# Handing the first DFT stage to the second by one-partition SBUF-to-SBUF DMAs instead of through DRAM

## The chip, the cores and the metric

The kernel runs on one core of one Trainium2 chip. The metric is the device time of one execution in microseconds (us). The median of three timed executions before the change is 1575.53 us (1574.32 to 1576.95). A difference below about 0.2% (3 us) can't be told from no change.

## The reference

Two blocks follow each other: a filter along the sequence, done in the frequency domain, and a gated feed-forward network.

```python
# x: (8, 3136, 256); filt_r, filt_i: (1569, 256)
X = np.fft.rfft(x, axis=1)
y = np.fft.irfft(X * (filt_r + 1j * filt_i)[None], n=3136, axis=1)
# w_in: (256, 1024), conv_w: (3, 1024), w_out: (1024, 256)
h = np.maximum(y @ w_in, 0)
conv_out = sum(conv_w[k] * hp[:, k:k + 3136] for k in range(3))   # hp: h with a zero row at both ends
out = (h * sigmoid(conv_out)) @ w_out
```

## The kernel before, in words

**The transform.** 3136 = 112 x 28, so the transform of a batch is made of matmuls with DFT tables. A *step* works on 2 of the 28 columns; 14 steps (`NP`) make a batch and 112 steps the eight batches. In one step there are:

- `first(b, p)`: loads rows of `x` (tile `x`, 112 x 512 floats, 224 KB), multiplies by `s1_sb` (two matmuls, L321), and `store("sa", ...)` copies the result from PSUM with ScalarE to the tile `sa` (L309) and sends it by a DMA on ScalarE's queue (L315) to the DRAM tensor `a_dram[b]`. A partition of `sa` holds one of 4 row kinds r and one of 28 groups g; the free axis has the 2 columns of the step.
- `second(b, p)`: needs, on the partitions, all 28 columns n and the 4 kinds r, and on the free axis the groups g. So `load("a", b, p)` reads `a_dram[b]` back in another order (on SyncE's queue, SP; L304), 2 groups a step. That is a turn of the data: each step of `second` needs something of every step of `first` of its batch. `second` multiplies by `s2_sb` (L328; in the last step of a batch L331) into PSUM `pp`.
- `filt(b, p)`: VectorE multiplies by the filter (L340 to L342), GpSimd adds (L344) into `z`.
- `third(b, p)`: multiplies `z` by `i1_sb` (L351); `store("sb", ...)` copies with ScalarE and sends it to `b_dram`.

`last_load`, `last_stage` and `last_out` bring `b_dram` back (tile `br`), make the last matmul (L216) and split the result in two parts, `y`, for the network. For batch 0 this happens at the end of this forward loop, for the others inside the network.

**The order.** One loop over `i` writes the instructions of PE, ACT, DVE and POOL in the order in which they run. In iteration `i` stand `first` of step `i - 1`, `second` of step `i - SKEW - 1`, `filt` of step `i - SKEW - 2` and `third` of step `i - SKEW - 4`, with `SKEW = NP + 4` = 18: the second stage runs 18 steps behind the first. DMAs on SP follow the order of the source as their waits allow. In the same loop, `x` is loaded 7 steps ahead, the tables and the filter are loaded in the first 26 iterations, and `convert_weights` turns the 64-bit weights into 32-bit pairs, a few instructions per iteration, in 8 chunks of 512 words from each weight tensor.

**DMA completions.** All DMAs of SP and ACT share eight completion semaphores, given out in turn (`DMAHW0` to `DMAHW7` in the rows below). A DMA that takes a semaphore waits until the DMA that had it before, eight places back in the order of both queues together, has landed.

**The network.** After the loop come the 28 chunks of the network (`inner`, `relu`, `conv`, `gate`, `split_g`, `project`), which fill the larger part of the span. The change doesn't touch them.

Of the kernel before, what the change touches and what calls it, by code (L numbers as in the profile page):

```python
# [9 lines left out]
F32 = mybir.dt.float32  # L10
F32R = mybir.dt.float32r
I32 = mybir.dt.int32
U32 = mybir.dt.uint32
AF = mybir.ActivationFunctionType
# [4 lines left out]
N2 = 28  # L19
G = 28  # L20
D = 256
# [17 lines left out]
def _dft_tables():  # L39
# [7 lines left out]
    n1, n2, c, a = np.arange(N1), np.arange(N2), np.arange(N2), np.arange(N1)  # L47
    s1 = np.zeros((N1, N2, 112))
    m2 = np.zeros((112, N1))
    i1 = np.zeros((2, 2, 28, G, N2, 4))  # L50
    for g in range(G):
        for s in range(2):
            if g == G - 1 and s == 1:
# [6 lines left out]
                for j in range(14):  # L60
                    if j:
                        w = np.conj(_w(j * c, N2))
                        i1[0, s, j, g, :, 2] = 2 * w.real
                        i1[1, s, j, g, :, 2] = -2 * w.imag
                    w = np.conj(_w((56 + 112 * j) * c, S))
# [4 lines left out]
            w = _w(k1 * (28 * n1[:, None] + n2[None, :]), S)  # L70
            s1[:, :, 2 * s * 28 + g] = w.real
            s1[:, :, (2 * s + 1) * 28 + g] = w.imag
            w = np.conj(_w(k1 * a, N1))
            m2[2 * s * 28 + g] = 2 * w.real / S
            m2[(2 * s + 1) * 28 + g] = -2 * w.imag / S
            for j in range(28):
                k2, sg = (j, 1) if j < 14 else (41 - j, -1)
                w = np.conj(_w((k1 + 112 * k2) * c, S))
# [5 lines left out]
    def s2(special):  # L84
        m = np.zeros((112, 2, 2, 28))
        for s in range(2):
            for j in range(28):
                if special and s == 1:
                    if j == 0:
                        m[n2 * 4 + 2, 0, s, 0] = 1.0  # L90
                        m[n2 * 4 + 2, 1, s, 0] = (-1.0) ** n2
                    else:
                        w = _w(n2 * j, N2) if j < 14 else _w(n2 * (56 + 112 * (j - 14)), S)
                        r = 2 if j < 14 else 3
                        m[n2 * 4 + r, 0, s, j] = w.real
                        m[n2 * 4 + r, 1, s, j] = w.imag
                    continue
                k2, sg = (j, 1) if j < 14 else (41 - j, -1)
                w = _w(n2 * k2, N2)
                m[n2 * 4 + 2 * s, 0, s, j] = w.real  # L100
                m[n2 * 4 + 2 * s + 1, 0, s, j] = -w.imag
                m[n2 * 4 + 2 * s, 1, s, j] = sg * w.imag
                m[n2 * 4 + 2 * s + 1, 1, s, j] = sg * w.real
        re, im, gap = m[:, 0].reshape(112, 56), m[:, 1].reshape(112, 56), np.zeros((112, 8))
        return np.concatenate([re, gap, im, -im, gap, re], 1)

    i1 = i1.reshape(2, 56, G, 112)
    i1 = np.concatenate([i1[0], np.zeros((8, G, 112)), i1[1]])
# [16 lines left out]
def tile_fft_filter_gated_ffn(  # L125
# [16 lines left out]
    nc = tc.nc  # L142
    B = x.shape[0]
# [35 lines left out]
        nc.tensor.matmul(ps, lhsT=wl, rhs=rh, start=False, stop=stop, **kw)  # L179

    dram = ctx.enter_context(tc.tile_pool(name="dram", bufs=1, space=bass.MemoryType.DRAM))
    a_dram = [dram.tile([N2, 112, D], F32, name=f"a_dram{b}") for b in range(B)]
    b_dram = [dram.tile([N2, 112, D], F32, name=f"b_dram{b}") for b in range(B)]

    wc = ctx.enter_context(tc.tile_pool(name="wc", bufs=1))
# [4 lines left out]
    wi = [wc.tile([128, KT, FF], F32R, name=f"wi{h}") for h in range(2)]  # L190
    wo = [wc.tile([128, NF, D], F32R, name=f"wo{h}") for h in range(2)]
# [33 lines left out]
    forward_pools = ExitStack()  # L225
    xp = forward_pools.enter_context(tc.tile_pool(name="xp", bufs=2, side="right"))
    s1_sb = xp.tile([112, N2, 112], F32, name="s1_sb", bufs=1)
    with (
        tc.tile_pool(name="fc", bufs=1) as fc,
        tc.tile_pool(name="fp", bufs=2) as fp,  # L230
# [3 lines left out]
        s2_sb = fc.tile([112, 120], F32, name="s2_sb")  # L234
        s2s_sb = fc.tile([112, 120], F32, name="s2s_sb")
# [5 lines left out]
        t1_sb = fc.tile([120, G, D], F32, name="t1_sb")  # L241
        t2_sb = fc.tile([120, G, D], F32, name="t2_sb")

        rows = {}

        def load_filter(c):
# [11 lines left out]
        raws = {}  # L258

        def load_weights(k):  # L260
            raws[k] = raw = cv.tile([128, 2, 512], I32, name="raw")
            for part, src in enumerate((w_in, w_out)):
                nc.sync.dma_start(out=raw[:, part], in_=src[:, 512 * k:512 * k + 512])

        def convert_conv():
            n = 3 * NF
            raw = cv.tile([128, 2, 512], I32, name="raw")
            nc.sync.dma_start(out=raw[:, 0, 0:2 * n], in_=conv_w)
            yield
            em = cv.tile([128, 2, 512], I32, name="em", bufs=1)  # L270
            yield from to_f32(cw.rearrange("p k f -> p (k f)"), raw[:, 0, 0:2 * n], em[:, 0, 0:n], em[:, 1, 0:n])

        def convert_weights():

            for k in range(8):
                raw = raws.pop(k)
                em = cv.tile([128, 2, 512], I32, name="em", bufs=1)
                ws = cv.tile([128, 2, 256], F32, name="ws")
                yield from to_f32(ws.rearrange("p t n -> p (t n)"), raw.rearrange("p t n -> p (t n)"), em[:, 0], em[:, 1])
                yield  # L280
                parts = [[t.rearrange("p a b -> p (a b)")[:, 256 * k:256 * k + 256] for t in w] for w in (wi, wo)]
                for part, (wh, wl) in enumerate(parts):
                    hi_act(wh, ws[:, part])
                yield
                for part, (wh, wl) in enumerate(parts):
                    lo_pool(wl, ws[:, part], wh)
                    yield
                if k < 6:
                    load_weights(k + 2)

        NP = 14
        parts = {}
        psums = {}

        def pool(kind):
            return xp if kind in ("x", "sa") else fp

        def load(kind, b, p):
            r = pool(kind).tile([112, 2, D], F32, name=kind, bufs=8 if kind == "x" else 5)
            if kind == "x":  # L300
                v = x[b].rearrange("(p n) d -> p n d", n=N2)
            else:
                v = a_dram[b].rearrange("n (r g) d -> (n r) g d", g=G)
            nc.sync.dma_start(out=r, in_=v[:, 2 * p:2 * p + 2])  # L304
            rows[kind, b, p] = r

        def store(kind, b, p, ps):
            st = pool(kind).tile([112, 2, D], F32, name=kind, bufs=4)
            nc.scalar.activation(st, ps, AF.Copy)  # L309
            sl = slice(2 * p, 2 * p + 2)  # L310
            if kind == "sa":
                v = a_dram[b][sl].rearrange("n p d -> p n d")
            else:
                v = b_dram[b].rearrange("n (r g) d -> (n r) g d", g=G)[:, sl]
            nc.scalar.dma_start(out=v, in_=st)  # L315

        def first(b, p):
            r = rows.pop(("x", b, p))
# [3 lines left out]
            return ps  # L322

        def second(b, p):
            r = rows.pop(("a", b, p))
            pp = fps.tile([120, 2, D], F32, name="pp", bufs=3)
            if p < NP - 1:
                nc.tensor.matmul(pp, lhsT=s2_sb, rhs=r, start=True, stop=True)  # L328
            else:
                for j, m in ((0, s2_sb), (1, s2s_sb)):  # L330
                    nc.tensor.matmul(pp[:, j], lhsT=m, rhs=r[:, j], start=True, stop=True)  # L331
            psums[b, p] = pp
# [21 lines left out]
        def at(i):  # L354
            return divmod(i, NP) if 0 <= i < NP * B else None

        SKEW = NP + 4
        nc.sync.dma_start(out=s1_sb[:, 0:4], in_=s1[:, 0:4])
        load("x", 0, 0)
        load("x", 0, 1)  # L360
        for c in range(1, 4):
            nc.sync.dma_start(out=s1_sb[:, 4 * c:4 * c + 4], in_=s1[:, 4 * c:4 * c + 4])
            load("x", 0, 2 * c)
            load("x", 0, 2 * c + 1)
        csteps, wsteps = convert_conv(), convert_weights()
        done = NP * B + 6
        NI = max(NP * B + SKEW + 5, done + N2 // 2 + 3)
        with tc.manual_schedule(engines=COMPUTE):
            for i in range(NI):
                f, m = i, i - SKEW  # L370
                if i == done:
                    forward_pools.close()
                    yps.append(ctx.enter_context(tc.tile_pool(name="y_even", bufs=1, side="right", reuse_waits="tile")))
                    lp = ctx.enter_context(tc.tile_pool(name="lp", bufs=2, side="right", reuse_waits="tile"))
                if 1 <= i < 4:
                    nc.sync.dma_start(out=s1_sb[:, 4 * i + 12:4 * i + 16], in_=s1[:, 4 * i + 12:4 * i + 16])
                if (bp := at(f + 7)) and i:
                    load("x", *bp)
                if bp := at(m + 3):
                    load("a", *bp)  # L380
                if i == 6:
                    nc.sync.dma_start(out=s2_sb, in_=s2[:, 0:120])
                    nc.sync.dma_start(out=s2s_sb, in_=s2s[:, 0:120])
                    nc.sync.dma_start(out=m2_sb, in_=m2)
                if 12 <= i < 26 and i % 2 == 0:
                    sl = slice((i - 12) // 2 * 4, (i - 12) // 2 * 4 + 4)
# [4 lines left out]
                pt = third(*bp) if (bp := at(m - 4)) else None  # L391
                pf = first(*bp) if (bp := at(f - 1)) else None
                if bp := at(m - 1):
                    second(*bp)
                if pt is not None:
                    store("sb", *at(m - 4), pt)
                if pf is not None:
                    store("sa", *at(f - 1), pf)
                if 3 <= i < 16:
                    next(csteps, None)  # L400
                if i == 16:
                    load_weights(0)
                    load_weights(1)
                if i >= 22 and i % 9 != 8:
                    next(wsteps, None)
                if 16 <= i < 30 and i % 2 == 0:
                    copy_filter(i // 2 - 8)
                c = 2 * (i - done)
# [113 lines left out]
                evacuate(*a)  # L522


PLAG = 6
AVOID = (3, 4, 5, 6, 7)
COMPUTE = {mybir.EngineType.PE, mybir.EngineType.Activation, mybir.EngineType.DVE, mybir.EngineType.Pool}
# [38 lines left out]
```

## Time and profile before

| What | Value |
|---|---|
| timed executions | 1574.32, 1575.53, 1576.95 us |
| span of the profiled execution | 1573.9 us (1.6 us below the median of the timed ones) |
| PE busy | 1510.8 us (96%) |
| DVE, ACT, POOL busy | 1280.7, 1192.6, 698.0 us |
| mean granted clock of TensorE | 0.984 |
| HBM read, written | 88.03 MB, 77.07 MB |
| `a_dram<-sa`, `a<-a_dram` | 112 DMAs each, 224 KB each |

The profile shows one execution. Its span runs from the first to the last instruction; what lies around it in a timed execution is the difference to the time. An engine's busy time is no bound by itself: the forward stage (to about 385 us) and the network (from there) have different limits and are read apart. For a DMA, "issue" is the time that the issuing queue (SPq, ACTq) spends on the instruction, and "landing" the time from the issue's start to the completion.

### The profile page before, as it was taken

Reading aid. Unit: us, or ns where it says so; the run is one execution under the profiler, and the core shown is the slowest. Engines: PE = TensorE matmul, PEld = TensorE weight load, DVE = VectorE, ACT = ScalarE, POOL = GpSimd, SP = SyncE. Lnnn points to the kernel's source line nnn. Section 1 sums busy time; section 2 is a strip of 40 time slices with the busy share of each in tenths; the row PEclk is TensorE's granted clock in tenths of the full one; section 3 lists DMA queues with packets and bytes.
Section 4 is the critical chain, followed back from the end, with each engine's and each line's share of the span. In section 5 each row is a group of like instructions: output and inputs, shape, how many; then the busy total and the mean of one; then the engine's idle time right before and its main releaser. Section 6 shows DMA issues by size and latency. Waiting matters only on the chain.

```text
span 1573.9 us, 26330 instructions
## 1 busy us (share of the span) xinstructions
PE 1510.8 (96%) x9424; PEld 1351.0 (86%) x9424; DVE 1280.7 (81%) x1965; ACT 1192.6 (76%) x2162; POOL 698.0 (44%) x624
## 2 busy tenths in 40 slices
PE   5699999998999999999999999999999999999998
PEld 4366666656999999999999999999999999999998
DVE  0487878897888888888888888888888888888887
ACT  3444444445988888888888888888888888888887
POOL 0255555562444444444444444444444444444444
PEclk8699999999999999999999999999999999999999
DMA  9999999984111011111111111111111111100001
GB/s 292 298 345 349 341 309 338 340 251 142 30 48 48 30 48 48 48 48 48 40 33 36 47 48 49 46 48 47 36 42 48 48 37 41 48 24 25 24 24 48
DMA packets 128278, 166.83 MB, mean 106 GB/s; under 512 B 10682, under 2 KB 87571, under 8 KB 128147
## 3 DMA queue, kind: packets, MB, share of 16 engines
q1 hardware_dynamic: 86931, 113.74, 23.1%
q10 hardware_dynamic: 41216, 51.39, 9.9%
q8 instruction: 75, 1.23, 0.3%
q14 instruction: 56, 0.46, 0.1%
HBM read 88.03 MB, written 77.07 MB: 105 GB/s over the span
## 4 chain that ended last, share of the span: by engine, by line
PE 83%; DMA 9%; DVE 4%; ACT 2%; issue 1%; ACTq 0%; POOL 0%; SPq 0%; DVEq 0%; POOLq 0%
PE ps_h L178 12%; PE ps_h L179 12%; PE ps_h L177 11%; PE po L473 11%; PE po L475 11%; PE po L474 11%; PE ps_h L216 5%; PE ps L321 4%; DMA x<-in_x 3%; PE ps L351 3%; PE pp L328 3%; DMA a<-a_dram 2%; DMA a_dram<-sa 2%; DVE y L149 1%; DVE v L341 1%
## 5 line engine op out<-in xcount | busy, mean ns | idle before, releaser
L152 POOL TENSOR_TENSOR g<-t,g 128x448 fp32r<-128x448 f32 x448 | 517.6, 1156 | 667.6 <-ACT g L146 265.8
L473 PE MATMUL po<-wo,g 128*128 128x256 f32 x1568 | 441.5, 282 | 0.0
L475 PE MATMUL po<-wo,g 128*128 128x256 f32 x1568 | 433.8, 277 | 0.0
L474 PE MATMUL po<-wo,g 128*128 128x256 f32 x1568 | 433.4, 276 | 0.0
L447 DVE SCALAR_TENSOR_TENSOR t<-ps_h,cw,t 128x448 f32<-128x448 f32 x448 | 305.5, 682 | 83.9 <-ACT t L442 73.3
L178 PE MATMUL ps_h<-y,wi 128*128 128x450 f32 x896 | 330.8, 369 | 4.2 <-DVE y L149 4.2
L177 PE MATMUL ps_h<-y,wi 128*128 128x450 f32 x896 | 329.2, 367 | 3.4 <-ACT y L146 2.1
L179 PE MATMUL ps_h<-y,wi 128*128 128x450 f32 x896 | 329.2, 367 | 0.0
L448 DVE SCALAR_TENSOR_TENSOR t<-ps_h,cw,t 128x448 f32<-128x448 f32 x448 | 306.4, 684 | 16.0
L442 ACT ACTIVATE t<-ps_h,cw 128x448 f32<-128x448 f32 x448 | 285.2, 637 | 42.1 <-ACT ps_h L440 0.7
L473 PEld LDWEIGHTS po<-wo,g 128*128 128x128 f32 x1568 | 294.7, 188 | 7.0
L474 PEld LDWEIGHTS po<-wo,g 128*128 128x128 f32 x1568 | 294.3, 188 | 5.7
L475 PEld LDWEIGHTS po<-wo,g 128*128 128x128 f32 x1568 | 294.4, 188 | 0.0
L440 ACT ACTIVATE ps_h<-ps_h 128x450 f32<-128x450 f32 x448 | 251.6, 562 | 32.5 <-PE ps_h L179 27.7
L453 DVE TENSOR_TENSOR t<-ps_h,t 128x448 f32<-128x448 f32 x448 | 275.1, 614 | 0.1
L452 ACT ACTIVATE t<-t 128x448 f32<-128x448 f32 x448 | 255.1, 569 | 12.2 <-DVE t L448 11.0
L146 ACT ACTIVATE g<-t 128x448 fp32r<-128x448 f32 x448 | 254.4, 568 | 0.2 <-DVE t L453 0.2
L344 POOL TENSOR_TENSOR z<-u,v 120x512 f32<-120x512 f32 x112 | 157.2, 1404 | 169.5 <-DVE v L342 144.8
L177 PEld LDWEIGHTS ps_h<-y,wi 128*128 128x128 f32 x896 | 170.4, 190 | 12.0 <-ACT y L146 3.3
L179 PEld LDWEIGHTS ps_h<-y,wi 128*128 128x128 f32 x896 | 168.6, 188 | 13.9
L178 PEld LDWEIGHTS ps_h<-y,wi 128*128 128x128 f32 x896 | 168.6, 188 | 13.5 <-DVE y L149 6.6
L149 DVE TENSOR_TENSOR y<-ps_h,y 128x448 fp32r<-128x448 f32 x98 | 103.1, 1052 | 76.7 <-ACT y L146 76.7
(51 smaller groups left out, 1447.5 us busy)
## 6 DMA issues: line engine op xcount, KB each, us to landing
x<-in_x SPq DMA_DIRECT2D x112, 224.0 KB, 4.6
a_dram<-sa ACTq DMA_DIRECT2D x112, 224.0 KB, 4.5
a<-a_dram SPq DMA_DIRECT2D x112, 224.0 KB, 4.7
b_dram<-sb ACTq DMA_DIRECT2D x112, 224.0 KB, 4.1
br<-b_dram SPq DMA_DIRECT2D x112, 224.0 KB, 2.6
out<-ot SPq DMA_DIRECT2D x27, 896.0 KB, 4.1
raw<-in_w_in SPq DMA_DIRECT2D x8, 256.0 KB, 4.6
raw<-in_w_out SPq DMA_DIRECT2D x8, 256.0 KB, 5.3
```

Of the source, the lines that this page charges most:

```text
L152: nc.gpsimd.tensor_tensor(out=dst, in0=src, in1=hi.bitcast(F32), op=ALU.subtract)
L177: nc.tensor.matmul(ps, lhsT=wh, rhs=rh, start=start, stop=False, **kw)
L178: nc.tensor.matmul(ps, lhsT=wh, rhs=rl, start=False, stop=False, **kw)
L179: nc.tensor.matmul(ps, lhsT=wl, rhs=rh, start=False, stop=stop, **kw)
L442: nc.scalar.activation(t, h[:, 1:SUB + 1], AF.Copy, scale=cw[:, 1, f:f + 1])
L447: nc.vector.scalar_tensor_tensor(out=t, in0=h[:, 0:SUB], scalar=cw[:, 0, f:f + 1], in1=t, op0=ALU.mult, op1=ALU.add)
L448: nc.vector.scalar_tensor_tensor(out=t, in0=h[:, 2:SUB + 2], scalar=cw[:, 2, f:f + 1], in1=t, op0=ALU.mult, op1=ALU.add)
L452: nc.scalar.activation(t, t, AF.Sigmoid)
L453: nc.vector.tensor_mul(t, h[:, 1:SUB + 1], t)
L473: nc.tensor.matmul(o, lhsT=gh[:, sl], rhs=wo[0][:, f], start=first, stop=False, skip_group_check=True)
L474: nc.tensor.matmul(o, lhsT=gh[:, sl], rhs=wo[1][:, f], start=False, stop=False, skip_group_check=True)
L475: nc.tensor.matmul(o, lhsT=gl[:, sl], rhs=wo[0][:, f], start=False, stop=last, skip_group_check=True)
```

## The change

The DRAM tensors `a_dram` go. Two SBUF tiles, `a_even` and `a_odd` (112 x 28 x 256 floats each), hold a whole batch in the order that `second` needs, and `second` reads its two groups right out of them. `load("a", ...)` goes. After `first` has been copied to `sa`, the new `turn` issues eight DMAs for the step, one for each pair of column j and kind r: each takes 28 partitions of `sa`, 1 KB from each, and writes the 28 KB into one partition of the batch tile. Six of the eight go out on SP and two on ACT (`BY_SP = 6`). The row that a DMA writes is `14 * (2 * r + j) + p`, so the eight rows of a step are 14 partitions apart; the rows of the table `s2` are put in the same order. `SKEW` becomes `NP + 2`. To make room in SBUF, `x` has 7 buffers instead of 8 and is loaded 5 steps ahead, and the weights are converted in 16 chunks of half the size, two pieces an iteration.

```diff
-        return np.concatenate([re, gap, im, -im, gap, re], 1)
+        rows = np.array([14 * (2 * r + n % 2) + n // 2 for n in range(28) for r in range(4)])
+        out = np.zeros((112, 120))
+        out[rows] = np.concatenate([re, gap, im], 1)
+        return out
...
-    a_dram = [dram.tile([N2, 112, D], F32, name=f"a_dram{b}") for b in range(B)]
...
+    a_sb = [xp.tile([112, G, D], F32, name="a_even", bufs=1)]
...
+        a_sb.append(fc.tile([112, G, D], F32, name="a_odd"))
...
-            raws[k] = raw = cv.tile([128, 2, 512], I32, name="raw")
+            raws[k] = raw = cv.tile([128, 2, 256], I32, name="raw")
...
-            for k in range(8):
+            for k in range(16):
...
+        def store_a(b, p, ps):
+            st = xp.tile([112, 2, D], F32, name="sa", bufs=4)
             nc.scalar.activation(st, ps, AF.Copy)
-            sl = slice(2 * p, 2 * p + 2)
-            if kind == "sa":
-                v = a_dram[b][sl].rearrange("n p d -> p n d")
...
-            nc.scalar.dma_start(out=v, in_=st)
+            rows["sa", b, p] = st
+
+        def turn(engine, b, p, which):
+            for q in which:
+                j, r = divmod(q, 4)
+                row = 14 * (2 * r + j) + p
+                engine.dma_start(out=a_sb[b % 2][row:row + 1], in_=rows["sa", b, p][28 * r:28 * r + 28, j])
...
         def second(b, p):
-            r = rows.pop(("a", b, p))
+            r = a_sb[b % 2][:, 2 * p:2 * p + 2]
...
-        SKEW = NP + 4
+        SKEW = NP + 2
...
-        done = NP * B + 6
+        done = NP * B + 4
...
-                if (bp := at(f + 7)) and i:
-                    load("x", *bp)
-                if bp := at(m + 3):
-                    load("a", *bp)
+                if (bp := at(f + 5)) and i:
+                    load(*bp)
...
+                if bp := at(f - 2):
+                    turn(nc.sync, *bp, range(BY_SP))
+                    turn(nc.scalar, *bp, range(BY_SP, 8))
+                    del rows["sa", bp[0], bp[1]]
...
-                if i >= 22 and i % 9 != 8:
+                if i >= 22:
+                    next(wsteps, None)
                     next(wsteps, None)
...
+BY_SP = 6
...
-    nc = bacc.Bacc("TRN2", target_bir_lowering=False, num_devices=1)
+    nc = bacc.Bacc("TRN2", target_bir_lowering=False, num_devices=1, dynamic_dma_scratch_size=1024)
```

SP's queue in the middle of the forward stage, before: each step has one load of `x` and one of `a`. The names in brackets are what a row waits for: a completion semaphore, or an engine.

```order
L304 DMA x<-in_x 112x512 [waits DMAHW7_49,PE_49]
L304 DMA a<-a_dram_61 112x512 [waits DMAHW0_49,PE_49]
L304 DMA x<-in_x 112x512 [waits DMAHW2_49,PE_49]
L304 DMA a<-a_dram_61 112x512 [waits DMAHW4_49,PE_49]
L304 DMA x<-in_x 112x512 [waits DMAHW6_49,PE_49]
```

The same queue after (two steps):

```order
L301 DMA x<-in_x 112x512 [waits DMAHW5_49,PE_49]
L313 DMA a_odd<-sa 1x28x256 [waits DMAHW6_49,Activation_49]
L313 DMA a_odd<-sa 1x28x256 [waits DMAHW0_49]
L313 DMA a_odd<-sa 1x28x256 [waits DMAHW2_49]
L313 DMA a_odd<-sa 1x28x256 [waits DMAHW4_49]
L313 DMA a_odd<-sa 1x28x256 [waits DMAHW5_49]
L313 DMA a_odd<-sa 1x28x256 [waits DMAHW6_49]
L301 DMA x<-in_x 112x512 [waits DMAHW7_49,PE_49]
L313 DMA a_odd<-sa 1x28x256 [waits DMAHW0_49,Activation_49]
```

One load of `a` has gone out of each step and six small DMAs have come in, each of which waits for a completion semaphore; `x` now stands behind them.

ACT in the same place, before:

```order
L309 ACTIVATE sb<-ps 112x512 [waits PE_49]
L315 DMA b_dram_69<-sb 112x512 [waits DMAHW4_49,Activation_49]
L309 ACTIVATE sa<-ps 112x512 [waits PE_49]
L315 DMA a_dram_62<-sa 112x2x256 [waits DMAHW6_49,Activation_49]
```

ACT after:

```order
L313 DMA a_odd<-sa 1x28x256 [waits DMAHW5_49,Activation_49]
L313 DMA a_odd<-sa 1x28x256 [waits DMAHW7_49]
L317 ACTIVATE sb<-ps 112x512 [waits PE_49]
L318 DMA b_dram_61<-sb 112x512 [waits Activation_49]
L306 ACTIVATE sa<-ps 112x512 [waits DMAHW3_49,DMAHW4_49,DMAHW2_49,DMAHW6_49,DMAHW0_49,PE_49]
```

Two small DMAs with a wait each now stand ahead of the copy of `sb` in a step, and the copy of `sa` waits for the DMAs that read the same buffer four steps before.

More of the change, by code (lines that the diff above doesn't have):

```diff
@@ L260, in load_weights @@
         def load_weights(k):
-            raws[k] = raw = cv.tile([128, 2, 512], I32, name="raw")
+            raws[k] = raw = cv.tile([128, 2, 256], I32, name="raw")
             for part, src in enumerate((w_in, w_out)):
-                nc.sync.dma_start(out=raw[:, part], in_=src[:, 512 * k:512 * k + 512])
+                nc.sync.dma_start(out=raw[:, part], in_=src[:, 256 * k:256 * k + 256])
         def convert_conv():
             n = 3 * NF
-            raw = cv.tile([128, 2, 512], I32, name="raw")
+            raw = cv.tile([128, 2, 256], I32, name="raw")
             nc.sync.dma_start(out=raw[:, 0, 0:2 * n], in_=conv_w)
             yield
-            em = cv.tile([128, 2, 512], I32, name="em", bufs=1)
+            em = cv.tile([128, 2, 256], I32, name="em", bufs=1)
             yield from to_f32(cw.rearrange("p k f -> p (k f)"), raw[:, 0, 0:2 * n], em[:, 0, 0:n], em[:, 1, 0:n])
         def convert_weights():
-            for k in range(8):
+            for k in range(16):
                 raw = raws.pop(k)
-                em = cv.tile([128, 2, 512], I32, name="em", bufs=1)
-                ws = cv.tile([128, 2, 256], F32, name="ws")
+                em = cv.tile([128, 2, 256], I32, name="em", bufs=1)
+                ws = cv.tile([128, 2, 128], F32, name="ws")
                 yield from to_f32(ws.rearrange("p t n -> p (t n)"), raw.rearrange("p t n -> p (t n)"), em[:, 0], em[:, 1])
                 yield
-                parts = [[t.rearrange("p a b -> p (a b)")[:, 256 * k:256 * k + 256] for t in w] for w in (wi, wo)]
+                parts = [[t.rearrange("p a b -> p (a b)")[:, 128 * k:128 * k + 128] for t in w] for w in (wi, wo)]
                 for part, (wh, wl) in enumerate(parts):
@@ L287, in convert_weights @@
                     yield
-                if k < 6:
+                if k < 14:
                     load_weights(k + 2)
@@ L293, in tile_fft_filter_gated_ffn, with load, store_b @@
         psums = {}
[L295 to L308, printed above, removed]
-            nc.scalar.activation(st, ps, AF.Copy)
-            sl = slice(2 * p, 2 * p + 2)
-            if kind == "sa":
-                v = a_dram[b][sl].rearrange("n p d -> p n d")
-            else:
-                v = b_dram[b].rearrange("n (r g) d -> (n r) g d", g=G)[:, sl]
-            nc.scalar.dma_start(out=v, in_=st)
+        def load(b, p):
+            r = xp.tile([112, 2, D], F32, name="x", bufs=7)
+            nc.sync.dma_start(out=r, in_=x[b].rearrange("(p n) d -> p n d", n=N2)[:, 2 * p:2 * p + 2])
+            rows["x", b, p] = r
+        def store_a(b, p, ps):
+            st = xp.tile([112, 2, D], F32, name="sa", bufs=4)
+            nc.scalar.activation(st, ps, AF.Copy)
+            rows["sa", b, p] = st
[4 more added lines that the diff above has]
+                engine.dma_start(out=a_sb[b % 2][row:row + 1], in_=rows["sa", b, p][28 * r:28 * r + 28, j])
+        def store_b(b, p, ps):
+            st = fp.tile([112, 2, D], F32, name="sb", bufs=4)
+            nc.scalar.activation(st, ps, AF.Copy)
+            nc.scalar.dma_start(out=b_dram[b].rearrange("n (r g) d -> (n r) g d", g=G)[:, 2 * p:2 * p + 2], in_=st)
         def first(b, p):
@@ L355, in at @@
             return divmod(i, NP) if 0 <= i < NP * B else None
-        SKEW = NP + 4
+        SKEW = NP + 2
         nc.sync.dma_start(out=s1_sb[:, 0:4], in_=s1[:, 0:4])
-        load("x", 0, 0)
-        load("x", 0, 1)
-        for c in range(1, 4):
+        load(0, 0)
+        load(0, 1)
+        for c in range(1, 3):
             nc.sync.dma_start(out=s1_sb[:, 4 * c:4 * c + 4], in_=s1[:, 4 * c:4 * c + 4])
-            load("x", 0, 2 * c)
-            load("x", 0, 2 * c + 1)
+            load(0, 2 * c)
+            load(0, 2 * c + 1)
         csteps, wsteps = convert_conv(), convert_weights()
-        done = NP * B + 6
+        done = NP * B + 4
         NI = max(NP * B + SKEW + 5, done + N2 // 2 + 3)
@@ L374, in tile_fft_filter_gated_ffn @@
                     lp = ctx.enter_context(tc.tile_pool(name="lp", bufs=2, side="right", reuse_waits="tile"))
-                if 1 <= i < 4:
-                    nc.sync.dma_start(out=s1_sb[:, 4 * i + 12:4 * i + 16], in_=s1[:, 4 * i + 12:4 * i + 16])
-                if (bp := at(f + 7)) and i:
-                    load("x", *bp)
-                if bp := at(m + 3):
-                    load("a", *bp)
+                if 1 <= i < 5:
+                    nc.sync.dma_start(out=s1_sb[:, 4 * i + 8:4 * i + 12], in_=s1[:, 4 * i + 8:4 * i + 12])
+                if (bp := at(f + 5)) and i:
+                    load(*bp)
                 if i == 6:
-                    nc.sync.dma_start(out=s2_sb, in_=s2[:, 0:120])
-                    nc.sync.dma_start(out=s2s_sb, in_=s2s[:, 0:120])
+                    nc.sync.dma_start(out=s2_sb, in_=s2)
+                    nc.sync.dma_start(out=s2s_sb, in_=s2s)
                     nc.sync.dma_start(out=m2_sb, in_=m2)
@@ L394, in tile_fft_filter_gated_ffn @@
                     second(*bp)
+                if bp := at(f - 2):
+                    turn(nc.sync, *bp, range(BY_SP))
+                    turn(nc.scalar, *bp, range(BY_SP, 8))
+                    del rows["sa", bp[0], bp[1]]
                 if pt is not None:
-                    store("sb", *at(m - 4), pt)
+                    store_b(*at(m - 4), pt)
                 if pf is not None:
-                    store("sa", *at(f - 1), pf)
+                    store_a(*at(f - 1), pf)
                 if 3 <= i < 16:
```

## The prediction, made before the changed kernel was run

> **What bounds the kernel now.** I read the page's slices first, since the change touches one stage only.
>
> ```profile
> span 1573.9 us, 26330 instructions
> ...
> PE   5699999998999999999999999999999999999998
> ...
> PEclk8699999999999999999999999999999999999999
> DMA  9999999984111011111111111111111111100001
> GB/s 292 298 345 349 341 309 338 340 251 142 30 48 48 30 48 48 48 48 48 40 33 36 47 48 49 46 48 47 36 42 48 48 37 41 48 24 25 24 24 48
> ```
>
> A slice is 39 us. The DMA digits stand at 8 or 9 for nine slices, to about 350 us, and fall to 1 when the network starts. PE stands at 9 from the third slice on. So whatever this change does, it does in the first quarter of the span; the network (about 1185 us) stays as it is. The middle of the forward stage in the view by windows, and after it in the view by tile the DMAs' issue times (ns, least/median/most) and the start of the first and last one:
>
> ```profile
> core 0: us, PE busy (x) PEld busy (x) DVE busy (x) ACT busy (x) POOL busy (x), PEclk, DMA share, GB/s
> 80.00:320.00 240.00, 224.72 (x845) 148.45 (x844) 196.69 (x296) 106.04 (x183) 135.56 (x104) 0.99 1.01 336
> ```
>
> ```profile
> L315 ACTq DMA_DIRECT2D a_dram<-sa x112: 311/312/1102, 7.1 to 327.6; - x112
> L304 SPq DMA_DIRECT2D a<-a_dram x112: 303/311/1352, 38.3 to 359.5; - x112
> L315 ACTq DMA_DIRECT2D b_dram<-sb x112: 310/321/386, 60.4 to 383.7; - x112
> ```
>
> The 112 stores of `sa` run from 7.1 to 327.6 us: 320.5 / 111 = 2.89 us a step. The window therefore holds 240 / 2.89 = 83 steps, and a step takes PE 224.72 / 83 = 2.71 us, DVE 2.37, ACT 1.28, POOL 1.63. The DMA engines are at a share of 1.01 with 336 GB/s: four transfers of 224 KB a step (0.917 MB / 2.89 us = 317 GB/s, and the rest weights and filters). So two things are at their limit together, the DMA engines and, 0.18 us below, PE. What the step waits for is shown by the waits of SP's own queue between 80 and 340 us (total, times, longest):
>
> ```profile
> SPq L304 <- PE ps L321: 55.6, 46, 2.2
> SPq L304 <- PE pp L328: 29.0, 30, 2.5
> SPq L304 <- DMA x<-in_x: 25.5, 31, 2.4
> SPq L304 <- DMA a<-a_dram: 22.9, 29, 3.6
> SPq L304 <- DMA a_dram<-sa: 20.0, 16, 3.4
> ```
>
> SP waits some 85 us for PE to free a buffer and some 68 us for DMAs (the first two rows, the last three). Both sorts are there: when DMAs are late PE stands, and the other way round. The stage would gain at most what lies between 2.89 and 2.71 us a step if all DMA trouble went.
>
> **What goes.** Two 224 KB transfers a step, 51.4 MB in all, and SP's one issue of `a` (0.31 us). On the DMA engines three transfers of 224 KB stay a step instead of four, one of them now from SBUF to SBUF. If bytes were all that counts, a step would need 3 x 0.229 MB / 336 GB/s = 2.05 us of them, which is under PE's 2.71.
>
> **What comes: issue time.** A step issues 7 DMAs on SP (`x`, six of `turn`) and 3 on ACT (`sb`, two of `turn`). Rows for one issue:
>
> ```profile
> L256 SPq DMA_DIRECT2D t_sb<-in_nyq x1: 229/229/229, 89.2 to 89.2; - x1
> ```
>
> ```profile
> 15.01 0.31 SPq L304 DMA_DIRECT2D x<-in_x  x1
> 15.37 0.43 SPq L376 DMA_DIRECT2D s_sb<-in_s  x1
> ```
>
> The only one-partition DMA (1 KB) took 0.23 us to issue, a large one 0.31, and the next one began 0.36 us after the one before. I take 0.36: SP needs 7 x 0.36 = 2.5 us a step, ACT 1.28 + 3 x 0.36 - these issues don't count as busy - = 2.4 us. Both stay under PE's 2.71, but SP goes from a queue with much spare time to one with 0.2 us of it. At 0.23 an issue SP would need 2.0 us. No cost on the path by itself.
>
> **What comes: the wait for a completion.** All DMAs share eight completion semaphores in turn, so at most eight are in flight. Before, a step had 4 DMAs, so a DMA had two steps (5.8 us) to land. Now a step has 10 and a DMA has 0.8 of a step. The step can't be shorter than the sum of the ten times to landing divided by 8. What a DMA takes to land, when the queues are full and when they are less so (medians of the DMA view: the page, then the windows 360 to 380 us at 172 GB/s, and 320 to 345 us at 234 GB/s):
>
> ```profile
> x<-in_x SPq DMA_DIRECT2D x112, 224.0 KB, 4.6
> ...
> out<-ot SPq DMA_DIRECT2D x1, 128.0 KB, 2.2
> ```
>
> ```profile
> br<-b_dram SPq DMA_DIRECT2D x7, 224.0 KB, 2.7
> b_dram<-sb ACTq DMA_DIRECT2D x6, 224.0 KB, 2.2
> ```
>
> ```profile
> b_dram<-sb ACTq DMA_DIRECT2D x10, 224.0 KB, 2.9
> a<-a_dram SPq DMA_DIRECT2D x10, 224.0 KB, 3.5
> ```
>
> After the change some 0.69 MB move in a step of about 3.3 us, 208 GB/s, between the two windows: I take 2.5 us for `sb` and 3.1 for `x`, 5.6 together. For one of the eight small ones no row exists, so from both sides. Low: the store of 224 KB in the quiet window lands in 2.2 us, of which 0.229 MB / 336 GB/s = 0.7 is transfer; 1.5 is left, and 28 KB at full rate add 0.1: 1.6 us. With the half of the 0.7 us that lie between the two windows for load, 1.95. High: all 28 KB go into one partition. If a partition takes them no faster than one DMA engine moves data (336 / 16 = 21 GB/s), that is 1.37 us instead of 0.1; on the 128 KB row's base (2.2 - 0.4 = 1.8) it makes 3.2, and with load 3.55. I take 2.5: the rows nearest to it in path and size of a packet give 1.95, and some of the one-partition cost must be paid, though eight DMAs go to eight partitions and can overlap.
>
> [...]
>
> **The sum.** (5.6 + 8 x 2.5) / 8 = 3.2 us, and 0.05 us between a landing and the next issue (the gap between the two issues above), ten times a step over eight, makes 3.26; I say 3.3. That is 0.41 us more than 2.89, times 112 steps: +46 us. `SKEW` falls by 2, so the tail after the last `first` has two iterations less. That tail ran from 327.6 to some 386 us, 23 iterations of 2.5 us: -5 us. Start-up: before, 18 iterations passed before `second` began, now 16, but SP has 16 x 2.5 = 40 us of issues in them plus some 30 loads of tables and filters at about 0.4 us, 52 us; 18 x 2.89 = 52. Nothing gained there. Forecast +41 us on the span of 1573.9 us, which lies 1.6 us below the median; on the median, 1616.5 us.
>
> **Edits at nothing.** The weights in 16 chunks: DVE's seven pieces and POOL's and ACT's few come twice as often at half the size.
>
> ```profile
> L168 DVE SCALAR_TENSOR_TENSOR ws<-em 128x512 f32<-128x512 int32 x7 | 4.8, 693 | 0.2
> L170 DVE TENSOR_SCALAR em<-ws 128x512 int32<-128x512 int32 x7 | 3.0, 428 | 0.2
> ```
>
> Seven such pieces a chunk are 7 x 0.43 to 7 x 0.69, about 4 us, and 8 chunks 32 us. If a half took as long as a whole (the worst), 32 us more over some 95 iterations: DVE at 2.37 + 0.34 = 2.71 us a step, still under 3.3. That cover is gone if the step falls to 2.7: then DVE is level with PE. `x` 5 steps ahead instead of 7 is 16 us ahead, against 3 us to land. The row order of `s2` changes no instruction. `turn` of a batch's first step waits for `second` of the last step two batches before, behind which `x` is queued; PE is ahead of SP when SP sets the pace, so I give it nothing. In the other case it costs a fraction of a step, eight times. Who waits when a small DMA is late: on ACT the copies of `sb` and `sa` behind it, for these PE, which has five PSUM buffers to run ahead.
>
> **Rivals.**
> - *The hand-over is fast (faster).* If a small DMA lands in 1.95 us, the sum gives (5.6 + 15.6) / 8 + 0.06 = 2.7 us, and PE with 2.71 sets the step. 96 steps past start-up x 0.18 = 17 us, and the tail's 5: -22, so about 1555 us. For it: the DMA engines' need falls from a share of 1.0 to 2.05 / 2.71 = 0.76, so landings shorten for all, and the wait for `a_dram` goes. Against it: 10 landings a step on 8 semaphores leave 2.1 us each, and no row is lower than 2.2. It decides below a landing of about 2.2 us, where the step is 2.94 and the loss is just the tail's 5 us.
> - *No change.* Landings of 2.1 to 2.2 us, or a step held at 2.9 by SP's issues with its waits: within 3 us of 1575.5.
> - *The small DMAs go one after the other (much slower).* If a small DMA is spread over many engines which all write the same partition, and the next one comes behind it on the same engines, none may overlap; then a step takes 8 x 1.37 = 11 us, and the kernel (11 - 2.89) x 112 = 910 us more. Against it: eight different partitions, and SP issues them 0.36 us apart, so engines that are done can go on. [...]
>
> **How the numbers follow.** Slower by a step of 3.0 to 4.3 us: 0.52, with the likeliest at 1616 us and a range of its own of 1585 to 1728. One after the other: 0.05. Fast hand-over: 0.37. No change: 0.06. So faster 0.37, same 0.06, slower 0.57. The range from 1553 (PE's floor) to 1720 us (a landing of 3.5) leaves out the case of one after the other, the top of the slow case and a gain beyond the floor.
>
> **What would show it.** [...] I am wrong if the small DMAs land in under 2.2 us, or if the start-up, which I hold at 52 us, gets much shorter because the stores to DRAM no longer compete with the loads there.

## The result, and the profile after

The changed kernel takes 1986.3 us (median of four, 1981.9 to 1988.9) against 1576.2 us: 1.260 times as long, interval 1.258 to 1.262. The forecast was 1616 us, with a range to 1720. The sign was right, the size was not: +410 us instead of +41. The page of the profile after, its span and slices (50 us each):

```profile
span 1983.9 us, 27237 instructions
...
PE   4165647475645538999999999999999999999999
...
PEclk6576778676877769999999999999999999999999
DMA  4455444344444435011111111111111111110101
```

The forward stage now fills 16 slices, 800 us. PE mostly stands at 4 to 7 there, and the DMA engines at 4 instead of 9: neither is at a limit. The granted clock of PE is lower there too (0.75 between 150 and 700 us), but PE is busy for 311 of these 550 us, and SP's own waits for PE add up to 3.5 us in them, so a slow PE isn't what SP waits for. The view by tile shows the issues of the small DMAs on SP and the copies of `sa`:

```profile
L313 SPq DMA_DIRECT2D a_even<-sa x336: 741/756/1534, 9.0 to 657.9; - x168
L306 ACT ACTIVATE sa<-ps x112: 597/597/598, 6.2 to 725.0; 112x512 f32<-112x512 f32 x112
...
L301 SPq DMA_DIRECT2D x<-in_x x112: 312/369/638, 1.2 to 700.0; - x112
```

The copies start 718.8 / 111 = 6.48 us apart (before: 2.89). One small DMA takes 0.756 us to issue, where a large one before took 0.31. SP's timeline in the middle of the stage (start, length):

```profile
409.63 0.37 SPq L301 DMA_DIRECT2D x<-in_x  x1
410.10 4.79 SPq L313 DMA_DIRECT2D a_even<-sa  x6
415.46 0.34 SPq L301 DMA_DIRECT2D x<-in_x  x1
415.90 4.74 SPq L313 DMA_DIRECT2D a_even<-sa  x6
```

Six issues fill 4.8 us, 0.80 us each with the gap, and the step is 5.8 us long although SP hardly waits in it. What it waits for between 150 and 700 us (84 steps):

```profile
SPq L301 <- DMA a_odd<-sa: 22.9, 25, 2.0
SPq L313 <- DMA b_dram<-sb: 20.9, 6, 4.4
SPq L301 <- DMA a_even<-sa: 17.1, 19, 1.9
```

All rows of this view make 92 us, 1.1 us a step. So of a step of 6.5 us in that window about 4.5 are issues of small DMAs, 0.5 the issues of `x` and of the weights, 0.4 gaps, and 1.1 waits. The whole +410 us is 3.59 us a step times 111 = 398, and 12 us in the tail: from the last `sa` to the last `sb` 68 us now (725.0 to 793.1), 56 before. The page holds no time to landing for the small DMAs of this kernel, so whether they land in under 2.2 us, where the prediction calls itself wrong, can't be read from it.

Some of the waits stand at one place: `second` of a batch's first step needs the last small DMA of the batch, and SP is behind. PE stood from 368.1 to 388.5 us ahead of that `second` (L331), and the matmuls of L354 and L324 that follow it in the program ran only after it, from 390.3. VectorE's timeline at such a place (the bracket is the idle time before):

```profile
362.85 0.69 DVE L345 TENSOR_TENSOR v<-pp,t_sb 56x512 f32<-56x512 f32 x1
390.63 0.69 DVE L343 TENSOR_TENSOR u<-pp,t_sb 120x512 f32<-120x512 f32 x1 [27.09 <-PE pp L331]
```

For 27 us the second stage stands; `sa` stands there for one step of 11 to 12 us in each batch.

### The profile page after: what moved, and what is told of

Read it like the earlier page. It is cut to its first block, busy times and chain, and to the rows that moved or that the text cites. A ratio compares the mean times of both kernels' runs of the same rounds, so it can differ in the third digit from the quotient of the medians.

```text
span 1983.9 us, 27237 instructions
## 1 busy us (share of the span) xinstructions
PE 1611.3 (81%) x9424; PEld 1382.6 (70%) x9424; DVE 1322.9 (67%) x2021; ACT 1193.2 (60%) x2178; POOL 689.5 (35%) x648
## 4 chain that ended last, share of the span: by engine, by line
PE 59%; DVE 2%; SPq 1%; DMA 1%; ACT 1%; issue 1%; ACTq 0%; POOL 0%; DVEq 0%; POOLq 0%
PE ps_h L181 9%; PE ps_h L182 9%; PE ps_h L180 9%; PE po L479 9%; PE po L481 9%; PE po L480 9%; PE ps_h L218 4%; SPq L313 1%; DVE y L152 1%; DMA a_odd<-sa 1%; ACT y L149 0%; DVE v L344 0%; DVE u L343 0%; PE ps L354 0%; PE pp L331 0%
## 5 line engine op out<-in xcount | busy, mean ns | idle before, releaser
L343 DVE TENSOR_TENSOR u<-pp,t_sb 120x512 f32<-120x512 f32 x112 | 77.5, 692 | 417.6 <-PE pp L331 325.7
L347 POOL TENSOR_TENSOR z<-u,v 120x512 f32<-120x512 f32 x112 | 145.5, 1301 | 449.2 <-DVE v L345 382.9
L306 ACT ACTIVATE sa<-ps 112x512 f32<-112x512 f32 x112 | 66.9, 597 | 389.6 <-DMA a_even<-sa 174.3
L446 ACT ACTIVATE ps_h<-ps_h 128x450 f32<-128x450 f32 x448 | 251.8, 562 | 32.1 <-PE ps_h L182 27.5
L324 PE MATMUL ps<-x,s_sb 112*112 112x256 f32 x448 | 162.9, 502 | 86.7 <-ACT sb L317 41.7
L354 PE MATMUL ps<-z,i_sb 120*112 120x256 f32 x448 | 145.9, 456 | 94.8 <-ACT sa L306 51.7
```

## The experiments

Theory A: SP's issue time of the small DMAs sets the step. Rivals: B, traffic makes the issues long; C, eight DMAs in flight and their landings set the step; D and E, the writes into one partition do; later F to I on single points, each named where it comes up.

**The shapes alone (e1_micro).** A kernel of nothing but DMAs.

```diff
+ for _ in range(6): nc.sync.dma_start(out=dst[0:1], in_=src[0:28, 0])       # L23: 28 rows into 1 partition
+ ... 16 rows (L25), 14 (L27), 8 (L29), 4 (L31); 28 into 28 partitions (L33); 112 into 112 (L35)
+ ... 28 rows DRAM -> 1 partition (L39); 28 SBUF -> DRAM (L41); L23 on ACT (L47)
+ for k in range(8): nc.sync.dma_start(out=dst[k:k + 1], ...)                # L51: eight neighbours; L49: 14 apart
```

> A kernel of DMAs alone; the transform and the network are left out. Six DMAs of each shape, each waiting for the landing of the one before, so that the rows give the issue time of a shape and the start-to-start time (landing plus hand-over); then eight of 28 rows to partitions 14 apart, and eight to neighbouring partitions. Theory A (the issue of this shape costs 0.75 us because of its shape): issue of 28 partitions into one stays at 0.74 to 0.78 us with nothing else going on. If it goes by the number of rows, 16, 14, 8, 4 rows give about 0.5, 0.45, 0.35, 0.3; if by the count not being a multiple of 16, 16 rows give 0.31 and 28 into 28 partitions stays at 0.75; if by the one partition on one side, 28 into 28 gives 0.31. Rival B (the issue is long because the queue is held up by DMA traffic in the full kernel): 0.31 here for every shape. Landing: 1.6 to 3.2 us by the prediction.

The view by line: issue time in ns (least/median/most), and the start of the first and the last of six (of eight for L49 and L51).

```profile
L23 SPq DMA_DIRECT2D dst<-src x6: 764/764/922, 16.5 to 39.0; - x6
L25 SPq DMA_DIRECT2D dst<-src x6: 502/503/583, 41.7 to 52.2; - x6
L27 SPq DMA_DIRECT2D dst<-src x6: 764/764/797, 54.2 to 65.5; - x6
L29 SPq DMA_DIRECT2D dst<-src x6: 634/634/652, 67.8 to 77.4; - x6
L31 SPq DMA_DIRECT2D dst<-src x6: 572/572/587, 79.3 to 87.9; - x6
L33 SPq DMA_DIRECT2D dst<-src x6: 746/746/804, 89.6 to 99.6; - x6
L35 SPq DMA_DIRECT2D dst<-src x6: 511/511/557, 101.6 to 112.4; - x6
L39 SPq DMA_DIRECT2D dst<-big x6: 716/724/768, 129.9 to 144.3; - x6
L41 SPq DMA_DIRECT2D big<-src x6: 306/307/340, 147.3 to 154.3; - x6
L47 ACTq DMA_DIRECT2D dst<-src x6: 763/764/1332, 190.5 to 204.4; - x6
L49 SPq DMA_DIRECT2D dst<-src x8: 747/760/818, 207.2 to 213.3; - x8
L51 SPq DMA_DIRECT2D dst<-src x8: 747/754/762, 214.1 to 219.7; - x8
```

B falls: 0.764 us with nothing else going on. The issue time doesn't go by the number of rows (14 cost as much as 28, 16 less) nor by the one partition (28 into 28: 0.746). With the destination in SBUF, 16 and 112 rows take 0.50 and 0.51, 28 and 14 rows 0.72 to 0.76, 8 rows 0.63, 4 rows 0.57; 28 rows into DRAM take 0.31. None of the three rules in the expectation fits all of these numbers (16 rows were to take 0.31 if only multiples of 16 were cheap), so what in the shape sets the issue time stays open. The start-to-start time of 28 rows into one partition is 13.9 / 5 = 2.78 us (on ACT, L47; the first DMA of L23 runs beside the large copy issued just before it, so its six can't be used whole), into 28 partitions 2.00, 14 rows into one 2.26. So 14 rows more (14.3 KB) into one partition, at the same issue time, cost 0.52 us, 27.5 GB/s. Eight DMAs to partitions 14 apart (L49) start 0.87 us apart, eight to neighbours (L51) 0.80: both lie near the issue time (0.760 and 0.754) and far under the 2.78 us of a DMA that waits for the one before it, so these starts don't tell the two cases apart.

**Four and five of the eight on SP (e2_bysp4, e11_bysp5).**

```diff
-BY_SP = 6
+BY_SP = 4        # e11: 5
```

> Four of the eight small DMAs on each queue instead of six and two. Theory A (SP's issues set the step): SP needs 4 x 0.81 + 0.45 = 3.7 us a step instead of 5.3, ACT 4 x 0.82 + 0.36 + 1.2 = 4.8, so the step falls from 6.5 to about 5 and the time to 1800 to 1850 us. Rival C (eight DMAs in flight, landings set the step): the number and size of DMAs are the same, so the step stays at 6.5 and the time at 1970 to 2000.

> Five of the eight small DMAs on SP, three on ACT. Theory A: between the two other splits, with SP's issues and gaps at 0.81 us a step less than with six: 1895 to 1935 us, unless ACT's 3 x 0.81 + 1.9 us a step hold it, which they don't by 0.3 us. Rival (the split with six is the best that issues allow, and four gained through something else): 1970 us or more.

With four: 1881.6 us (1.194, 1.184 to 1.205). With five: 1974.9 us (1.253, 1.249 to 1.257). Four gains 105 us, in the way of A, though 30 us less than it expected at least. Five gains 11 us, where A expected 50 at least: the number lies with the rival, and SP's issues alone don't set the step: with five they and their gaps fill 4.7 us of a step of 6.4, with four 3.9 of 5.6 (counted in the traces between 150 us and the last steps). With four the long step at the start of each batch is gone too, with five it isn't. The view by tile and, from the timelines of ACT and SP, one step with five:

```profile
L306 ACT ACTIVATE sa<-ps x112: 597/597/598, 6.4 to 717.1; 112x512 f32<-112x512 f32 x112
```

```profile
405.86 0.60 ACT L306 ACTIVATE sa<-ps 112x512 f32<-112x512 f32 x1 [3.23 <-DMA a_even<-sa]
406.48 2.54 ACTq L313 DMA_DIRECT2D a_even<-sa  x3
```

```profile
404.07 3.98 SPq L313 DMA_DIRECT2D a_even<-sa  x5
410.17 0.36 SPq L267 DMA_DIRECT2D raw<-in_w_in  x1
```

ACT's copy waits 3.2 us for small DMAs of SP; then ACT issues three of its own, and SP, done at 408.05, stands until 410.1. The trace names a landing of a small DMA as what it waited for; ACT was the queue that had just issued some. I read it as two queues that hold each other up; e13 below takes the small DMAs off ACT.

**Neighbouring partitions (e3_adjacent).**

```diff
-                row = 14 * (2 * r + j) + p
+                row = 8 * p + 4 * j + r            # and the rows of s2 in that order
```

> The eight rows of a step are neighbouring partitions (8p to 8p + 7) instead of 14 apart, with the table in the same order. Theory A (issue time on SP sets the step): no change, 1970 to 2000 us, issue 0.75 us. [...]

2136.5 us (1.356, 1.347 to 1.366): 150 us more than the changed kernel at the same issue time (median 0.756). A, which expected no change, is wrong here, and D, by which the writes set the step, is nearer: the step grows from 6.5 to 7.8 us, and ACT's copies of `sa` stand 438 us in all for small DMAs, against 332 in the changed kernel. That rows 14 apart land sooner is my reading of these waits; no landing time is behind it.

**Half the rows, at the same and at a shorter issue time (e4_rows14, e5_rows16).**

```diff
-  engine.dma_start(out=a_sb[b % 2][row:row + 1], in_=rows["sa", b, p][28 * r:28 * r + 28, j])
+  engine.dma_start(out=a_sb[b % 2][row:row + 1, 0:14], in_=rows["sa", b, p][28 * r:28 * r + 14, j])   # e5: 16
```

> Each small DMA carries 14 of the 28 rows (half of the data of the second stage is left out; the batch tiles are set to zero at the start). Alone, 14 rows take the same 0.76 us to issue as 28 and land 0.52 us sooner (start to start 2.25 us against 2.77). Theory A (issue time on SP sets the step, landings add some 1 us of waits to it): the issue part of 5.4 us stays and only the waits shrink, by 0.3 to 0.8 us a step: 1895 to 1950 us. Rival C (landings and the bytes into one partition set the step): ten landings shorter by 8 x 0.52 / 8 = 0.5 us a step at least, and half the bytes halves what is over 2.9 us: 1780 to 1850 us.

> Each small DMA carries 16 of the 28 rows (12 groups of 28 are left out of the second stage's data; the batch tiles are set to zero at the start). Alone, 16 rows take 0.50 us to issue where 14 and 28 take 0.76, with a landing like that of 14 rows (2.07 us start to start). Theory A: against the 14-row kernel six issues a step on SP are 0.26 us shorter each, 1.56 us a step: 160 to 180 us less than it. Rival C: within 30 us of the 14-row kernel, since it moves 2 KB more a DMA and lands 0.2 us sooner.

14 rows: 1935.1 us (1.226, 1.223 to 1.229), 51 us less than with all rows. 16 rows: 1848.4 us (1.171, 1.169 to 1.174), 87 us less again with 14% more bytes. The issue times in the view by tile, 14 rows first:

```profile
L315 SPq DMA_DIRECT2D a_even<-sa x336: 741/756/2138, 9.1 to 612.2; - x168
```

```profile
L315 SPq DMA_DIRECT2D a_even<-sa x336: 502/581/1073, 9.1 to 537.8; - x168
```

Half the bytes and landings 0.5 us shorter (alone, 2.26 us start to start against 2.78) give 51 us, what A expected and not C. The step from 14 to 16 rows lies between the two forecasts, A's 160 to 180 us and C's 30. Six issues 0.175 us shorter each (1.05 us a step, 118 us in all) give 87: about three quarters of it reach the end, the rest comes back as waits. A's 160 us came from the 0.50 us of the shape alone; in the kernel the issue takes 0.58. The page of the 16-row kernel, unlike that of the changed one, also holds the times to landing:

```profile
x<-in_x SPq DMA_DIRECT2D x112, 224.0 KB, 3.1
b_dram<-sb ACTq DMA_DIRECT2D x112, 224.0 KB, 2.5
a_even<-sa SPq DMA_DIRECT2D x336, 16.0 KB, 2.2
```

`x` and `sb` land in just the 3.1 and 2.5 us that the prediction took, and a small DMA of 16 rows in 2.2. Ten such landings over eight completions are (5.6 + 8 x 2.2) / 8 = 2.9 us; the step is 5.3 us long (from the copies of `sa`). So that sum isn't what sets it.

**28 partitions instead of one (e7_spread).**

```diff
-  engine.dma_start(out=a_sb[b % 2][row:row + 1], ...)
+  engine.dma_start(out=a_sb[b % 2][28 * r:28 * r + 28, 2 * p + j], ...)
```

> The eight small DMAs of a step keep number, size, queues and their 28 source partitions, but write 28 partitions, 1 KB each, instead of one (a copy without the turn, so the second stage gets its data in the wrong place). Alone, this shape takes 0.75 us to issue, as before, and lands 0.79 us sooner (1.98 us start to start against 2.77). Theory A (issues of 0.76 us on SP set the step, landings add about 1 us of waits): the 5.4 us of issues and gaps stay, the waits shrink to 0.2 to 0.6 us: 1880 to 1930 us. Rival E (the one partition at the far end is what costs): the step falls to the 3.3 us of the prediction or below, 1580 to 1640 us.

1901.8 us (1.207, 1.204 to 1.210): 84 us less, as A expected; E falls. All that SP still waits for between 150 and 620 us makes 16 us, 0.2 us of a step of 5.7, and no row is a small DMA; the largest:

```profile
SPq L312 <- ACT sa L306: 6.7, 13, 0.7
SPq L301 <- PE ps L323: 5.3, 17, 0.5
```

Here SP does almost nothing but issue, and the step is as long as that takes. The 84 us are not all the price of the one partition. Without the turn, `second` needs only the small DMAs of its own step, so the long step at the start of each batch is gone as well (14 copies of `sa` take 80 us instead of 91); six such steps, each some 5.5 us over the others, are about 33 of the 84 us.

**Into DRAM, with a short issue (e10_to_dram).**

```diff
-  engine.dma_start(out=a_sb[b % 2][row:row + 1], ...)
+  engine.dma_start(out=a_dram[b][row:row + 1], ...)
```

> The small DMAs keep number, queues, order and 28 KB each, but write a row of a DRAM tensor instead of a partition of SBUF; the second stage reads zeros (its data is left out). Alone, 28 rows from SBUF to DRAM take 0.31 us to issue, against 0.76, and land and hand over in 1.40 us. Theory A: SP's issues and gaps fall to 6 x 0.36 + 0.55 = 2.7 us a step, so the step falls to the 3.2 us that VectorE's weights set, or the 3.3 of the prediction's own sum: 1590 to 1640 us. Rival C (ten DMAs a step with eight completions set the step, whatever their issue takes): not below 1700 us.

1709.9 us (1.085, 1.082 to 1.088). The view by tile, and what SP waits for between 100 and 420 us:

```profile
L316 SPq DMA_DIRECT2D a_dram<-sa x672: 306/380/1101, 11.8 to 471.3; - x168
L309 ACT ACTIVATE sa<-ps x112: 597/597/599, 6.3 to 462.4; 112x512 f32<-112x512 f32 x112
```

```profile
SPq L316 <- DMA b_dram<-sb: 35.5, 37, 2.2
SPq L316 <- DMA a_dram<-sa: 16.2, 19, 2.1
```

Three things together take away 276 of the 410 us: the shorter issue, the shorter landing that comes with it, and that `second`, which reads zeros, no longer waits for the small DMAs at the start of a batch. This run doesn't tell them apart. But the step is 456.1 / 111 = 4.11 us, not 3.2: SP, with 3.2 us of issues and gaps in a step (six of 0.38, `x` 0.33, weights 0.2, gaps 0.4), waits for completions, most of all for those held by `sb`. Here C's bound of 1700 us held and A's 1640 didn't. What is left, 134 us over the kernel before, has the weights in it (15 to 20 us in the kernel before, below). The rest I put down to SP's 3.2 us and to its waits for landings, about 66 us in the window or 0.9 us a step. The sum of ten landings over eight doesn't explain these: with 1.4 us for a small DMA (its time alone) it gives 2.1 us.

**All eight on SP; more buffers for `sa` (e13_bysp8, e12_sa6).**

```diff
-BY_SP = 6
+BY_SP = 8
```

```diff
-            st = xp.tile([112, 2, D], F32, name="sa", bufs=4)
+            st = xp.tile([112, 2, D], F32, name="sa", bufs=6)      # x: 5 buffers, loaded 4 steps ahead
```

> All eight small DMAs on SP. SP's issues and gaps are 8 x 0.81 + 0.55 = 7.0 us a step. Theory H: without small DMAs on ACT there is little left to wait for, the step is 7.0 to 7.4 us: 2040 to 2090 us. Rival I: the wait of 1 us a step stays, 7.9 to 8.2 us: 2140 to 2180 us.

> The changed kernel with six buffers for sa instead of four (and five for x, loaded 4 steps ahead, to make room). Theory H (the 1 us a step over SP's issues comes from the two queues waiting for each other: ACT's copy of sa waits for SP's small DMAs of four steps before, and SP for the completion that a small DMA of ACT holds): with two steps more of slack the waits shrink by 0.3 us a step or more, 1890 to 1955 us. Rival I (the waits are landings that no buffer can hide, eight in flight being the limit): 1970 to 2000 us.

All eight on SP: 2104.3 us (1.334, 1.327 to 1.340), between the two ranges, 14 us above H's. The issue time is the same 0.761 us, and SP's waits between 150 and 700 us shrink to three rows of note:

```profile
SPq L313 <- DMA b_dram<-sb: 12.5, 5, 2.9
SPq L301 <- DMA b_dram<-sb: 11.4, 5, 3.0
SPq L267 <- DMA b_dram<-sb: 3.1, 1, 3.1
```

No small DMA makes SP wait any more, which points to ACT's small DMAs as the larger part of the waits of 1 us a step. Six buffers for `sa`: 2025.2 us in the profiled execution, 39 us slower (a second timing, 4106 us, stands alone and isn't explained, so there is no ratio). Both forecasts failed: steps inside a batch stay, and the copies of `sa`, which now run up to six steps ahead of SP, stand 22 us instead of 11 at each batch's start, where PE waits for `second`. The slack moves the wait; it doesn't remove it. Both edits change a second thing (the split of the issues; the loads of `x`), so how the 1 us divides between buffers, completions and landings stays open.

**The side edits (e6_side, e8_weights, e9_x).** The kernel before with the change's other edits: all, the weights alone, `x` alone.

```diff
-            for k in range(8):                    # 512 words a chunk
+            for k in range(16):                   # 256 words a chunk; e8 has this part alone
...
-                if i >= 22 and i % 9 != 8:
+                if i >= 22:
+                    next(wsteps, None)
                     next(wsteps, None)
...
-  bufs=8 if kind == "x" else 5    ...  at(f + 7)
+  bufs=7 if kind == "x" else 5    ...  at(f + 5)  # e9 has this part alone
```

> The kernel before, with its DRAM round trip, and the change's other edits alone: weights in 16 chunks of half the size with two pieces an iteration, 7 buffers of x loaded 5 steps ahead. My prediction costed them at nothing: 1570 to 1580 us. Rival: they lengthen the forward stage, by up to 0.34 us a step on DVE or by late loads of x: 1585 to 1615 us.

> The kernel before with the weights in 16 half-size chunks, two pieces an iteration, alone. Theory F (VectorE's pieces set the pace: 3.0 us a step of DVE in the side-edits kernel against 2.37): 1588 to 1598 us, all of the 15 us. Rival G (x loaded later costs it): 1574 to 1580 us.

> The kernel before with 7 buffers of x, loaded 5 steps ahead, alone. Theory F: within 5 us of before. Rival G: 1588 to 1598 us.

All: 1593.0 us (1.0098, 1.0081 to 1.0115). Weights: 1596.0 us (1.0132, 1.0106 to 1.0158). `x`: 1575.3 us (0.9992, 0.9978 to 1.0006). So F: the weights cost 15 to 20 us in the kernel before. In the window from 80 to 320 us of the weights kernel (PE, PEld, DVE, ACT, POOL):

```profile
80.00:320.00 240.00, 207.39 (x761) 133.87 (x759) 222.19 (x318) 96.61 (x178) 118.16 (x115) 0.98 0.96 310
```

VectorE is busy for 222 of 240 us (197 before) and is now the fullest engine; that it, and not the twice as many loads of weights, costs the 15 to 20 us is read from this trace and not tested apart. Its timeline, and GpSimd's beside it:

```profile
209.34 0.69 DVE L342 TENSOR_TENSOR v<-pp,t_sb 56x512 f32<-56x512 f32 x1
210.06 0.43 DVE L164 TENSOR_TENSOR em<-em 128x256 int32<-128x256 int32 x1
210.52 1.24 DVE L166 TENSOR_SCALAR em<-raw 128x256 int32<-128x256 int32 x1
```

```profile
210.17 1.44 POOL L344 TENSOR_TENSOR z<-u,v 120x512 f32<-120x512 f32 x1 [1.18 <-DVE v L342]
```

The second piece of an iteration, half as large as before (where this piece took 0.43 us), ends at 211.76, just after GpSimd's `z` (211.61): 1.24 us. In the changed kernel the same piece (L169 there) took 0.29 us at 174.17, when it began 0.14 us before a `z` (174.31), and 1.24 us at 218.39, when it began inside one (218.05 to 219.49). In that kernel, with VectorE busy for 243 of the 550 us from 150 to 700, this should be hidden under a step of 6.5 us; no run tests it.

## Why the prediction was wrong

- **Issue time: the step that failed.** "I take 0.36 ... No cost on the path by itself." The two rows that I used were a DMA of one row of 1 KB (0.23 us) and loads of 112 rows from DRAM (0.31). Neither has 28 rows going into SBUF; the trace before had no such shape and I didn't bound its price from above, as I did for the landing. It is 0.76 us, 0.80 with the gap: SP needs 5.5 us a step (with the weights), not 2.5, and becomes the bound. The shapes alone show the 0.764. That it reaches the end is shown by 14 against 16 rows (87 us less with more bytes), by eight on SP (118 us more), and by the 28 partitions, where SP issues almost without a pause and the step is still 5.7 us. It isn't the whole: with six on SP about 1 us a step are waits, and with five or four SP's issues don't fill the step; how much of that is the two queues' order, the buffers or the landings stays open.
- **Landings: nearly right, as far as seen.** I took 2.5 us; alone it is 2.78 start to start, 0.05 of it hand-over by the prediction's estimate. In the changed kernel itself no landing was recorded; with 16 rows, `x` and `sb` land as I took them. With neighbouring partitions the kernel took 150 us more (e3), and ACT's copies of `sa` stood 106 us more for small DMAs; I put that down to the writes.
- **Ten landings on eight completions: not what set the step.** The sum divided by 8 is a lower bound, 3.3 us by the prediction, 3.5 with the 2.78 us from start to start alone, against 6.5. With a short issue (e10) it falls to 2.1, and the step was 4.1 us. Waits for completions are there, 0.9 us a step, but the sum doesn't give them; I suspect that handing them on in one order over two queues, of which each also waits for other things, costs more, and no run isolates it.
- **Weights at nothing: wrong by itself, probably without effect here.** I allowed DVE 0.34 us a step at worst; in the kernel before they bring it from 2.37 to 3.0. A half taking as long as a whole was no worst case: the piece that began inside GpSimd's `z` took longer than the whole did before (1.24 us against 0.43). `x` at nothing was right.
- **Tail and start-up.** -5 us was forecast for the tail, +12 came: SP is behind, and its last small DMA goes out at 744.0 us, 19 us after the last copy of `sa`. `second` began at 105 us instead of 45 before; I had held that equal.
- **Rivals.** "One after the other", the far case, was not what happened: DMAs to eight partitions 14 apart do overlap (eight in a step of 6.5 us, where each by itself needs 2.78), SP just issued one every 0.80 us. The fast rival had no chance with such an issue time.
- **The sign: luck in large part.** Slower was forecast for the wait for completions, and slower came from a term that was put at nothing.

No version with the small DMAs beats the kernel before.

## What to carry to other kernels

Price a DMA by three numbers: its issue on the queue, its landing, and its share of the DMA engines. Cutting a step's two large DMAs into eight small ones took the DMA engines from a share of 1.01 (80 to 320 us) to 0.43 (150 to 700 us), and lost 410 us, most of it because the queue that issues them was nearly full instead (5.4 of a step's 6.5 us). Before counting on a shape of DMA that the profile doesn't hold, issue six of it in a kernel of its own; it takes a few lines and shows both issue and landing.

## What the runs showed of the hardware

- Issue times of a DMA on SP (and ACT) depend on its shape: into SBUF 0.50 us for 16 rows and 0.51 for 112 from SBUF, 0.76 for 14 and for 28, 0.63 for 8, 0.57 for 4; into DRAM 0.31 for 28. The loads of 112 rows from DRAM in the kernel before took 0.31. Which property of the shape decides these runs don't show.
- 14 rows more (14.3 KB) into one partition took 0.52 us more from start to start, 27.5 GB/s; eight DMAs into neighbouring partitions made the kernel 150 us slower than into partitions 14 apart.
- A VectorE instruction from SBUF to SBUF (L166 of e8_weights) that began inside a GpSimd instruction on SBUF took 1.24 us and ended 0.15 us after it. In the changed kernel the same one took 0.29 us when it began 0.14 us before that of GpSimd, and 1.24 us when it began inside it; one twice as large took 0.43 us in the kernel before.
